# Last unit's single-quadrant products in two banks of their own, both last additions ahead of all copies, other units' sums folded in ahead of time

## Chip, cores, metric

One core of one Trainium2 chip. The metric is the device time of one execution in microseconds. Every run and every trace here is one execution of the whole program.

## The reference, cut to what matters

A gated recurrence over 4 sequences of 6,080 positions and 256 channels, then a two-layer block with `h - tanh(h)` between.

```python
def _attn_ref(x, f_logit, lower_bound):
    f = lower_bound + (1.0 - lower_bound) * sigmoid(f_logit)
    for t in range(S):
        h = f[:, t] * h + (1.0 - f[:, t]) * x[:, t]
        y[:, t] = h
    return y

def _moe_ref(x, w_in, w_out):          # x: (24320, 256), w_in: (256, 2048)
    h = x @ w_in
    g = h - np.tanh(h)
    return (g @ w_out).astype(np.float32)
```

## The kernel before

The program runs over 48 blocks of tokens (one of 256, then 512 each) and, in each, four units of 512 hidden channels. From the third block on, both layers use a fast matrix scheme with seven products in place of eight. The second layer's seven products are collected in four PSUM banks, `Qa` to `Qd`, over the four units; at the end of a block their sums are combined into the four quadrants `C[0]` to `C[3]` of the output, turned, and written. What the change touches is the end of the last block:

```python
PARTS = (
    (("Qa", 0, A11, "h", 0), ("Qa", 1, S1, "T", 0)),
    (("Qb", 0, A12, "h", 3), ("Qb", 1, S2, "h", 1)),
    (("Qc", 0, S3, "T", 1),),
    (("Qd", 0, S4, "h", 2), ("Qd", 1, A22, "T", 2)),
)

def finish(j, step):                       # p15, o1, o2, o3 (o4 only in other blocks)
    ...
    o, a, b = (
        None,
        (C[:, 0:2], acc[j, 1][:, :, 0:hb], twice(0)),
        (C[:, 2], acc[j, 2][:, 0, 0:hb], C[:, 1]),
        (C[:, 1:4:2], C[:, 1:3], twice(1)),
        (C[:, 1:3], acc[j, 3][:, :, 0:hb], C[:, 1:3]),
    )[step]
    nc.vector.tensor_tensor(out=o, in0=a, in1=b, op=ALU.add)

def end(j):                                # the last block's o4 and output
    ...
    for half in range(2):
        slot, r = ((2, 1), (1, 0))[half]
        nc.vector.tensor_tensor(
            out=C[:, slot], in0=acc[j, 3][:, r, 0:hb], in1=C[:, slot], op=ALU.add
        )
        name = ("Qa", "Qb")[half]
        bank = ps_b.tile([P, 2, KC, P], FP32, name=name, tag=name)
        for i in range(2):
            for k in range(KC):
                nc.tensor.transpose(
                    bank[:, i, k], C[:, 2 * k + half, i * P : (i + 1) * P], ident[:]
                )
        rows = osb[:, 2 * half : 2 * half + 2]
        (nc.scalar.copy, nc.vector.tensor_copy)[half](
            out=rows.rearrange("p i (m k) -> p i k m", k=KC), in_=bank[:]
        )
        t0 = starts[j] + half * hb
        nc.sync.dma_start(out=out[t0 : t0 + hb, :].rearrange(...), in_=rows)
```

The polynomial in place of `tanh` holds only for small arguments. The program therefore collects a flag, and after the fast path every engine reads the flag and jumps over a second, general path, which is unrolled over all 48 blocks. With these inputs the flag is zero and the path is never taken:

```python
fast()
seen = nc.values_load(flag[:].bitcast(INT32), ...)
with tc.If(seen != 0):
    general()
```

## Time and profile before

| | kernel before |
|---|---|
| median of the first 3 runs | 2330.94 us (2330.39 to 2331.64) |
| span of the profiled execution | 2330.1 us |
| TensorE busy | 2318.8 us, at full clock |
| last product of TensorE ends | 2322.83 us |
| from there to the end of the span ("tail") | 7.28 us |

The lines of the profile are in the prediction. In this trace TensorE has no gap between the opening (the first 12 us) and its last product, so only the 7.28 us behind that product can be won.

### The profile page before, as it was taken

What the parts mean: (1) busy time and instruction counts of PE and PEld (TensorE: products, weight loads), DVE (VectorE), ACT (ScalarE), POOL (GpSimd) and SP (SyncE); (2) the same over time, 40 slices, a digit from 0 to 9 for tenths busy, and PEclk for the clock granted to TensorE, in tenths of its full rate; (3) what the DMA queues carried; (4) which work ended last, traced back from release to release, by engine and by line L of the source; (5) the groups of instructions that cost most, each with busy time, mean ns of one, the idle gap of its engine ahead of it and who ended that gap; (6) DMA issues with size and microseconds to landing.
All of it is one profiled execution on the core that took longest, in us unless ns stands there. A gap on an engine that the chain in (4) does not pass through costs nothing.

```text
span 2330.1 us, 28649 instructions
## 1 busy us (share of the span) xinstructions
PE 2318.8 (100%) x10676; PEld 2025.3 (87%) x10676; DVE 2121.3 (91%) x2447; ACT 1800.6 (77%) x2686; POOL 0.7 (0%) x6
## 2 busy tenths in 40 slices
PE   9999999999999999999999999999999999999998
PEld 5888888888888888888888888888888888888887
DVE  8999899998999989999899999999899998999987
ACT  7777777777777777787777777777777777777775
POOL 0000000000000000000000000000000000000000
PEclk9999999999999999999999999999999999999999
DMA  6311211112111111111111121111211112111101
GB/s 172 64 23 29 45 37 28 28 33 41 37 28 28 37 37 37 28 28 40 33 37 28 28 44 30 37 28 28 46 28 37 28 28 46 31 33 28 28 10 29
DMA packets 296948, 85.05 MB, mean 36 GB/s; under 512 B 289888, under 2 KB 292704, under 8 KB 296800
## 3 DMA queue, kind: packets, MB, share of 16 engines
q1 hardware_dynamic: 296512, 82.87, 16.9%
q8 instruction: 85, 1.39, 0.3%
q14 instruction: 63, 0.52, 0.1%
q10 hardware_dynamic: 288, 0.26, 0.0%
HBM read 58.20 MB, written 24.90 MB: 36 GB/s over the span
## 4 chain that ended last, share of the span: by engine, by line
PE 99%; DMA 0%; DVE 0%; issue 0%; ACT 0%; SPq 0%
PE A L388 27%; PE Qd L471 14%; PE Qa L471 14%; PE D L388 14%; PE Qb L471 14%; PE B L388 7%; PE Qc L471 7%; PE A L687 1%; PE Qc L754 1%; PE Qa L754 1%; PE Qb L754 1%; PE D L687 0%; PE Qd L687 0%; PE B L687 0%; DMA fn<-in_f_logit_dram 0%; PE Qa L687 0%
## 5 line engine op out<-in xcount | busy, mean ns | idle before, releaser
L388 PE MATMUL A<-T,w_in 128*128 128x256 f32 x2208 | 558.8, 379 | 0.0
L388 PEld LDWEIGHTS A<-T,w_in 128*128 128x128 f32 x2208 | 419.5, 190 | 57.0
L432 DVE TENSOR_TENSOR h<-h,q 128x1024 f32<-128x1024 f32 x368 | 437.6, 1220 | 3.1
L426 DVE SCALAR_TENSOR_TENSOR q<-q,t 128x1024 f32<-128x1024 f32 x368 | 440.0, 1216 | 0.0
L419 ACT ACTIVATE q<-t 128x1024 f32<-128x1024 f32 x368 | 382.8, 1053 | 46.7 <-DVE h L432 43.8
L416 ACT ACTIVATE t<-h 128x1024 f32<-128x1024 f32 x368 | 388.6, 1056 | 3.1 <-DVE h L403 0.3
L437 ACT ACTIVATE junk<-t 128x1024 bf16<-128x1024 f32 x368 | 388.1, 1055 | 1.5
L451 DVE TENSOR_TENSOR Tg<-h 128x1024 f32<-128x1024 f32 x368 | 348.0, 946 | 6.4
L471 PE MATMUL Qb<-h,w_out 128*128 128x256 f32 x1472 | 347.7, 379 | 0.0
L471 PEld LDWEIGHTS Qb<-h,w_out 128*128 128x128 f32 x1472 | 279.7, 190 | 38.0
L471 PE MATMUL Qd<-h,w_out 128*128 128x256 f32 x736 | 219.0, 379 | 0.0
L471 PE MATMUL Qa<-Tg,w_out 128*128 128x256 f32 x736 | 219.0, 379 | 0.0
L471 PE MATMUL Qa<-h,w_out 128*128 128x256 f32 x736 | 218.9, 379 | 0.0
L471 PE MATMUL Qd<-Tg,w_out 128*128 128x256 f32 x736 | 218.9, 379 | 0.0
L400 ACT COPY h<-B 128x512 f32<-128x512 f32 x184 | 106.9, 581 | 143.0 <-PE B L388 94.2
L400 ACT COPY h<-A 128x512 f32<-128x512 f32 x184 | 107.2, 583 | 136.7 <-PE A L388 125.3
L403 DVE TENSOR_TENSOR h<-D,r 128x512 f32<-128x512 f32 x184 | 126.9, 689 | 92.7 <-PE D L388 89.1
L403 DVE TENSOR_TENSOR h<-A,r 128x512 f32<-128x512 f32 x184 | 126.3, 687 | 73.8 <-PE A L388 42.1
L400 ACT COPY r<-A 128x512 f32<-128x512 f32 x184 | 107.2, 583 | 105.9 <-PE A L388 105.9
L388 PE MATMUL D<-T,w_in 128*128 128x256 f32 x736 | 188.9, 379 | 0.0
L388 PE MATMUL A<-y,w_in 128*128 128x256 f32 x736 | 188.9, 379 | 0.0
L388 PE MATMUL B<-y,w_in 128*128 128x256 f32 x736 | 188.9, 379 | 0.0
(120 smaller groups left out, 3069.2 us busy)
## 6 DMA issues: line engine op xcount, KB each, us to landing
xn<-in_x_dram SPq DMA_DIRECT2D x184, 128.0 KB, 3.3
fn<-in_f_logit_dram SPq DMA_DIRECT2D x184, 128.0 KB, 3.1
out_dram<-osb SPq DMA_DIRECT2D x180, 128.0 KB, 2.8
raw<-in_moe_w_out_dram SPq DMA_DIRECT2D x8, 512.0 KB, 4.9
raw<-in_moe_w_in_dram SPq DMA_DIRECT2D x7, 512.0 KB, 4.7
out_dram<-osb SPq DMA_DIRECT2D x3, 256.0 KB, 3.9
fn<-in_f_logit_dram SPq DMA_DIRECT2D x1, 512.0 KB, 7.3
xn<-in_x_dram SPq DMA_DIRECT2D x1, 512.0 KB, 8.2
```

The source lines that it names most:

```text
L388: nc.tensor.matmul(ps[:, c], lhsT=w_in[u][:, slot, c * P : (c + 1) * P], rhs=mixes[j][right], start=start and c == 0, stop=True, skip_grou ...
L400: nc.scalar.copy(out=dst, in_=piece(n, bank))
L403: nc.vector.tensor_tensor(out=piece(n, "h")[:, q], in0=piece(n, bank), in1=piece(n, r), op=ALU.add)
L416: nc.scalar.activation(out=half(n, i, "t"), in_=half(n, i), func=AF.Square)
L419: nc.scalar.activation(out=half(n, i, "q"), in_=half(n, i, "t"), func=AF.Square, scale=RA, bias=RB,)
L426: nc.vector.scalar_tensor_tensor(out=q, in0=q, scalar=RC, in1=t, op0=ALU.add, op1=ALU.mult)
L432: nc.vector.tensor_tensor(out=h, in0=h, in1=q, op=ALU.mult)
L437: nc.scalar.activation(out=junk[:, :, :, 0 : st[n]["hb"]], in_=t, func=AF.Relu, bias=-TINY, accum_out=flags[:, 2 * n + i : 2 * n + i + 1],)
L451: nc.vector.tensor_tensor(out=o, in0=a, in1=b, op=ALU.subtract)
L471: nc.tensor.matmul(acc[j, part][:, r, 0 : st[n]["hb"]], lhsT=w_out[u][:, slot, c * P : (c + 1) * P], rhs=piece(n, right)[:, q, c], start=( ...
L687: nc.tensor.matmul(h[c], lhsT=w_in[u][:, 2 * k + s, c * P : (c + 1) * P], rhs=ys[j][:, k, 0:nb], start=k == 0 and (c == 0 or len(banks) == 2),
L754: nc.tensor.matmul(acc[j][i // 2][:, i % 2].rearrange("p (k m) -> p k m", k=2), lhsT=plain[j, u][:, s, c, i * P : (i + 1) * P], rhs=w_out[ ...
```

## The change

The intent: make the last two additions start as early as possible. The last unit's two products that go into only one quadrant each (`A22`, `S4`) get a PSUM bank each, so that the addition of the first can start while TensorE is still on the second. The other units' sums in `Qd` are copied out before and folded in before the end. Both last additions stand ahead of all copies, and the copies out are halved and spread over four banks and two engines. The diff, cut to its core:

```diff
+        def part_end(j, step):
+            p, kept = acc[j, "p"][:, :, 0:hb], acc[j, "kept"]
+            if step == "o1":
+                finish(j, 1)
+            if step == "p15":
+                nc.vector.tensor_tensor(
+                    out=kept[:, 2], in0=p[:, 1], in1=kept[:, 0], op=ALU.add
+                )
+                return
+            for o, a, b in {
+                "o1": (),
+                "o2": ((kept[:, 3], acc[j, 2][:, 0, 0:hb], C[:, 1]),),
+                "o3": (
+                    (C[:, 2], kept[:, 3], kept[:, 1]),
+                    (C[:, 1], C[:, 1], kept[:, 2]),
+                    (C[:, 3], kept[:, 3], p[:, 1]),
+                ),
+            }[step]:
+                nc.vector.tensor_tensor(out=o, in0=a, in1=b, op=ALU.add)
 ...
         def end(j):
+            alone = [ps_a.tile([P, TB], FP32, name="A", tag="A")[:, 0:hb] for _ in range(2)]
+            for half, (slot, right, q) in enumerate(((A22, "T", 2), (S4, "h", 2))):
+                for c in range(2):
+                    nc.tensor.matmul(
+                        alone[half],
+                        lhsT=w_out[NU - 1][:, slot, c * P : (c + 1) * P],
+                        rhs=piece(n, right)[:, q, c],
+                        start=c == 0,
+                        stop=c == 1,
+                    )
             for half in range(2):
-                slot, r = ((2, 1), (1, 0))[half]
+                slot = 2 - half
                 nc.vector.tensor_tensor(
-                    out=C[:, slot], in0=acc[j, 3][:, r, 0:hb], in1=C[:, slot], op=ALU.add
-                )
-                name = ("Qa", "Qb")[half]
-                bank = ps_b.tile([P, 2, KC, P], FP32, name=name, tag=name)
+                    out=C[:, slot], in0=alone[half], in1=C[:, slot], op=ALU.add
+                )
+            for half in range(2):
                 for i in range(2):
-                    for k in range(KC):
+                    name = ("Qa", "Qb", "Qc", "D")[2 * half + i]
+                    bank = ps_b.tile([P, KC, P], FP32, name=name, tag=name)
+                    for k in (0, 1) if half == 0 else (1, 0):
                         nc.tensor.transpose(
-                            bank[:, i, k], C[:, 2 * k + half, i * P : (i + 1) * P], ident[:]
+                            bank[:, k], C[:, 2 * k + half, i * P : (i + 1) * P], ident[:]
                         )
-                (nc.scalar.copy, nc.vector.tensor_copy)[half](
-                    out=rows.rearrange("p i (m k) -> p i k m", k=KC), in_=bank[:]
-                )
+                    (nc.scalar.copy, nc.vector.tensor_copy)[i](
+                        out=osb[:, 2 * half + i].rearrange("p (m k) -> p k m", k=KC),
+                        in_=bank[:],
+                    )
 ...
+                    if final and (name, u) == ("Qd", NU - 2):
+                        kept = mixpool.tile([P, 4, HB], FP32, name="T")
+                        acc[j, "kept"] = kept
+                        nc.scalar.copy(
+                            out=kept[:, 0:2], in_=acc[j, 3][:, :, 0 : sizes[j] // 2]
+                        )
```

More of the change, by code (lines that the diff above doesn't have):

```diff
@@ L521, in give @@
                 )
+        def part_end(j, step):
+            hb = sizes[j] // 2
+            p, kept = acc[j, "p"][:, :, 0:hb], acc[j, "kept"]
[6 more added lines that the diff above has]
+                return
+            C = acc[j, "C"][:, 0 : 4 * hb].rearrange("p (n t) -> p n t", n=4)
+            for o, a, b in {
[8 more added lines that the diff above has]
+                nc.vector.tensor_tensor(out=o, in0=a, in1=b, op=ALU.add)
@@ L523, in end @@
         def end(j):
-            hb = sizes[j] // 2
+            hb, n = sizes[j] // 2, j * NU + NU - 1
             C = acc[j, "C"][:, 0 : 4 * hb].rearrange("p (n t) -> p n t", n=4)
             osb = opool.tile([P, NQ, D], FP32, name="osb", tag="osb")
+            alone = [ps_a.tile([P, TB], FP32, name="A", tag="A")[:, 0:hb] for _ in range(2)]
[8 more added lines that the diff above has]
+                    )
@@ L540, in end @@
                         )
-                rows = osb[:, 2 * half : 2 * half + 2]
-                (nc.scalar.copy, nc.vector.tensor_copy)[half](
-                    out=rows.rearrange("p i (m k) -> p i k m", k=KC), in_=bank[:]
-                )
+                    (nc.scalar.copy, nc.vector.tensor_copy)[i](
+                        out=osb[:, 2 * half + i].rearrange("p (m k) -> p k m", k=KC),
+                        in_=bank[:],
+                    )
                 t0 = starts[j] + half * hb
@@ L546, in end @@
                 nc.sync.dma_start(
-                    out=out[t0 : t0 + hb, :].rearrange("(i p) d -> p i d", p=P), in_=rows
+                    out=out[t0 : t0 + hb, :].rearrange("(i p) d -> p i d", p=P),
+                    in_=osb[:, 2 * half : 2 * half + 2],
                 )
@@ L903, in fast @@
                         continue
+                    final = j == NBLK - 1
+                    if final and (name, u) == ("Qd", NU - 1):
+                        continue
                     if u is None:
-                        if (name, j) == ("o1", NBLK - 1):
+                        if final and name == "o1":
                             nc.vector.reduce_max(
@@ L908, in fast @@
                             )
-                        if j == NBLK - 1 and name in ("o4", "otr"):
-                            if name == "o4":
-                                end(j)
+                        if final and name == "o3":
+                            sum_up()
+                        if final and name == "o4":
+                            end(j)
+                        if final and name[0] == "o":
+                            if name in ("o1", "o2", "o3"):
+                                part_end(j, name)
                             continue
-                        if (name, j) == ("o3", NBLK - 1):
-                            sum_up()
                         steps[name](j)
@@ L917, in fast @@
                             fetch(j + 1)
+                        if final and name == "p15":
+                            part_end(j, name)
                         continue
                     steps[name](j * NU + u)
+                    if final and (name, u) == ("Qd", NU - 2):
[4 more added lines that the diff above has]
+                        )
     @with_exitstack
```

## The prediction

> **What bounds the kernel now.** I read the page first: the busy time of each engine, then the granted clock in 40 slices.
>
> ```profile
> span 2330.1 us, 28649 instructions
> PE 2318.8 (100%) x10676; PEld 2025.3 (87%) x10676; DVE 2121.3 (91%) x2447; ACT 1800.6 (77%) x2686; POOL 0.7 (0%) x6
> PEclk9999999999999999999999999999999999999999
> ```
>
> TensorE is busy for all but 11 us at full clock, so only fewer matmuls, or less time in which nothing is left to multiply, can help. The change takes no matmul away before the last unit. It can only touch the tail, so I read the table of windows next, with a cut at 2322.85 us, where the last product ends (columns: stretch, its length, busy us of PE, PEld, DVE, ACT, POOL with counts, clock, DMA share, GB/s).
>
> ```profile
> 2315.00:2322.85 7.85, 7.85 (x38) 6.41 (x36) 5.97 (x9) 0.73 (x2) 0.00 (x0) 1.00 0.31 68
> 2322.85:2330.10 7.25, 1.14 (x8) 0.73 (x7) 1.45 (x3) 0.62 (x1) 0.00 (x0) 0.91 0.26 84
> ```
>
> Up to 2322.85 TensorE has no gap; 7.25 us follow. That is everything the change can win from, 0.3% of the time. The chain that ended last says what lies in it (start, length, what):
>
> ```profile
> 2320.91 1.94 PE Qd L471 x8
> 2322.85 0.02 issue
> 2322.87 0.44 DVE C L531
> 2323.31 0.04 issue
> 2323.35 0.55 PE Qa L538 x3
> 2323.90 0.51 PE Qb L538 x4
> 2324.41 0.02 issue
> 2324.44 0.69 DVE osb L542
> ```
>
> The products into bank Qd end; both last additions, each 256 columns, read that bank; transposes into Qa, then into Qb; the second copy out. From there the transfer view and the view of the DMA queue's waits take over:
>
> ```profile
> out_dram<-osb SPq DMA_DIRECT2D x2, 256.0 KB, 3.9
> SPq L1046 <- DMA out_dram<-osb: 2.0, 2, 1.4
> ```
>
> The records give the two issues at 2324.58 and 2325.16, just behind the copies that end at 2324.56 (ACT) and 2325.13 (DVE). The second transfer lands at 2329.04, and 1.07 us of closing waits and barriers make 2330.11. So the end is: second copy done, then 3.9 us, then 1.07 us.
>
> Last, the timeline of VectorE and ScalarE just ahead of the end:
>
> ```profile
> 2320.02 0.69 DVE L503 TENSOR_TENSOR C<-Qb,p 128x512 f32<-128x512 f32 x1 [0.72 <-issue]
> 2320.83 0.42 DVE L503 TENSOR_TENSOR C<-Qc,C 128x256 f32<-128x256 f32 x1
> 2321.29 0.69 DVE L503 TENSOR_TENSOR C<-C,p 128x512 f32<-128x512 f32 x1
> 2322.87 0.76 DVE L531 TENSOR_TENSOR C<-Qd,C 128x256 f32<-128x256 f32 x2 [0.89 <-PE Qd L471]
> 2318.24 0.59 ACT L487 COPY p<-Qa 128x512 f32<-128x512 f32 x1 [5.20 <-PE Qa L471]
> ```
>
> VectorE idles 0.89 us before the last additions, ScalarE 5.2 us before its copy. There is room for added work in both.
>
> **What the Trainium skill says.** "PSUM — Partial Sum Buffer", section "PSUM bank collisions raise a hardware error", says that two engines must not touch one bank (same partitions) at once, even in disjoint columns, and wants waits guarded by bank. The trace agrees in effect: both sums of Qd are read only after its last matmul (2322.83), though the first matmuls for either half were done well before; the additions start at 2322.87 and 2323.21. "VectorE: DVE Perf Modes", section "The TRN2 errata", gives (N+151)/0.96 ns for an fp32 tensor_tensor add: 424 ns for 256 columns, 691 for 512. The trace has 425 and 415, 692 and 693: it agrees, and I use it for the added additions. [...] "Runtime: NRT & Kernel Launch", section "Instruction fetch mechanics", says that a taken branch outside the fetched pages has to fetch instructions by DMA. At the end each engine branches over the second code path; the trace has a 16,384-byte instruction packet from 2325.44 for 1.36 us amid the output transfers. That matters for a rival below.
>
> **The change part by part.** The order of the built program differs only in the last few dozen instructions; TensorE has the same count of products and transposes.
>
> (a) ScalarE copies Qd's sums of the first three units to SBUF. They are complete at about 2314.96 (last start 2314.58 plus 0.379); the copy is 0.59 us as L487's, done by 2315.7, in the idle 5.2 us. Cost on the path: 0.
>
> (b) VectorE adds p's second half to the kept sum (0.425 us) behind p's copy (2318.24+0.59 = 2318.83): 2318.87 to 2319.30. The reduction (0.54 us) moves to about 2319.24 to 2319.78. Its reader on TensorE comes only after Qc's products, at 2320.72: 0.9 us of slack. The addition of Qb waits for Qb's products anyway (2320.02). Cost 0.
>
> (c) After Qb (unchanged, ends 2320.71) and Qc (starts 2320.83, ends 2321.25), the 512-column addition becomes three of 256. The first starts as before at 2321.29; independent ones follow at 0.341 us, as the two of L531 do (2322.872 to 2323.213): 2321.29, 2321.63, 2321.97.
>
> (d) TensorE makes the same eight matmul passes, but the four of A22 first, into their own bank, then the four of S4. The first bank is done at the fourth start 2321.591 plus 0.379 = 2321.97, 0.86 us before the second (2322.83). The first last addition starts when VectorE is free: 2321.97+0.34 = 2322.31, ends 2322.74. In the kernel before it ended at 2323.30: 0.56 us won. The second runs 2322.87 to 2323.30; before, 2323.21 to 2323.63: 0.33 won.
>
> (e) Transposes now come in four groups of two. C[0] is ready early (2322.67 as before). C[2] follows the first addition by 0.053 us: 2322.79, ending 2323.12 (the 0.331 us of the first one after a wait). Qb's two end at 2323.34 (steps of 0.17 and 0.11 us, then 0.273). Qc's C[3] needs nothing; its C[1] waits for the second addition: 2323.35, ending 2323.68. D's end at 2323.90. Before, the last transpose ended at 2324.40: 0.50 won.
>
> (f) Copies are halved and paired across engines. ScalarE needs about 0.38 us for 256 columns (0.617 less 256 at 0.92 ns, the slope between 583 ns for 512 and 1055 for 1024), VectorE about 0.425. ScalarE: 2323.16 to 2323.54, 2323.72 to 2324.10. VectorE: 2323.38 to 2323.80, 2323.94 to 2324.36. So the first issue falls at 2323.83 instead of 2324.58, the second at 2324.39 instead of 2325.16: 0.75 and 0.77 us won. Of the 0.77, 0.50 are from additions and transposes, 0.27 from the shorter last copy.
>
> If transfer and closing keep their 3.9 and 1.07 us, the span falls by 0.77 us.
>
> **The rivals.** First, *the exit holds part of it back*. In the records, most of the output's packets are through by 2327.3, but a thin stream goes on until 2328.6, and a lone DMA engine's 32 packets of 46 ns make 1.5 us; it looks as if one engine began only after the instruction packet ended at 2326.79. TensorE's branch follows its last transposes' dispatch, which moves by only some 0.4 us (2323.74 to 2323.35). If that fetch sets the straggler, 0.4 us is won, not 0.77. Against it: transfers that start 0.75 us earlier have more packets through before the fetch. It makes 2330.5.
>
> Second, *VectorE's chain becomes the bound*. If the three additions do not overlap, each takes 0.46 us with its wait; the first last addition starts at 2322.69, the second at 2323.15 and ends 2323.57, close to before (2323.63). Then the split copies alone win, some 0.3 us: 2330.6. Against it: the built program has no wait between the three.
>
> Third, *noise or a new stall*. A new wait of TensorE on its own counter stands before the S4 products, but for a value reached dozens of matmuls earlier; four banks instead of two mean more semaphore hops (some 0.04 us each). If these eat everything: 2330.9, no change.
>
> **Range and chances.** I weigh the full 0.77 and the exit's 0.4 about equally: 0.6 us off the median of 2330.94, 2330.3 us. The three runs before spread over 1.25 us, twice the gain; with that and 0.3 us for the mechanism the range is 2329.4 to 2331.2. A gain of 2% would be 47 us, and the whole tail is 7.25: faster by over 2% is out of reach at 0.003. For slower there is no mechanism of that size: 0.007. Within 2%: 0.99.
>
> **What would show it.** In the profile after, the first last addition should start near 2322.31 and the second near 2322.87; the last copy should end near 2324.36; the issues should stand near 2323.83 and 2324.39; the stretch from the last product's end to the end of the span should be about 6.5 us instead of 7.25 (6.9 if the exit holds it). I am wrong if the additions of L546 stand 0.46 us apart, if TensorE shows a gap before 2322.8, if either copy takes as long as the 512-column one, or if the second transfer takes clearly longer than 3.9 us from issue to landing. A time below 2329.4 would mean that the exit shrank with it, which I have no reason to expect.

## The result, and the profile after

| | before | after |
|---|---|---|
| median of 6 runs | 2331.81 us (2330.39 to 2332.45) | 2331.66 us (2329.70 to 2332.48) |
| ratio | | 0.9999, 95% interval 0.9987 to 1.0012 |
| tail of the profiled execution | 7.28 us | 7.44 us |

Ratios are the mean time of one kernel's fast runs over that of the other's of the same rounds, so they are not quite the ratio of the medians. The prediction of 2330.3 us, with a range to 2331.2, missed: the time lies 0.5 us above the range.

The page after, its span and its busy times:

```profile
span 2330.3 us, 28654 instructions
PE 2319.1 (100%) x10674; PEld 2025.5 (87%) x10676; DVE 2121.6 (91%) x2451; ACT 1801.5 (77%) x2688; POOL 0.7 (0%) x6
```

VectorE's timeline after (start, length, engine, line, operation, idle time before it and its releaser):

```profile
2321.27 0.43 DVE L546 TENSOR_TENSOR C<-T 128x256 f32<-128x256 f32 x1
2321.61 0.42 DVE L546 TENSOR_TENSOR C<-C,T 128x256 f32<-128x256 f32 x1
2321.95 0.42 DVE L546 TENSOR_TENSOR C<-T,p 128x256 f32<-128x256 f32 x1
2322.28 0.41 DVE L566 TENSOR_TENSOR C<-A,C 128x256 f32<-128x256 f32 x1
2322.85 0.42 DVE L566 TENSOR_TENSOR C<-A,C 128x256 f32<-128x256 f32 x1 [0.16 <-PE A L557]
2323.33 0.42 DVE L577 COPY osb<-Qb 128x256 f32<-128x256 f32 x1
2323.92 0.42 DVE L577 COPY osb<-D 128x256 f32<-128x256 f32 x1 [0.16 <-PE D L574]
```

The engines did what the change wants. The first last addition starts at 2322.28, while TensorE is still on its last products (before: 2322.87). The chain that ended last, after:

```profile
2320.89 1.92 PE A L557 x8
2322.82 0.26 PE Qa L574 x2
2323.08 0.22 PE Qb L574 x2
2323.30 0.37 PE Qc L574 x2
2323.66 0.23 PE D L574 x2
2323.90 0.02 issue
2323.92 0.42 DVE osb L577
```

No addition stands on the chain any more, and the last copy ends at 2324.35, 0.78 us before the 2325.13 of the kernel before. But the windows table, cut at the last product's end, and the transfers of the kernel after say that nothing of it arrives:

```profile
2322.82:2330.26 7.44, 1.06 (x8) 0.66 (x7) 1.27 (x3) 0.77 (x2) 0.00 (x0) 0.72 0.26 83
```

```profile
out_dram<-osb SPq DMA_DIRECT2D x2, 256.0 KB, 4.5
```

```profile
SPq L1096 <- DMA out_dram<-osb: 2.6, 2, 2.0
```

The tail is 7.44 us in place of 7.28. The transfers take 4.5 us from issue to landing in place of 3.9, and the closing wait for them is 2.6 us in place of 2.0. What was won ahead of the transfers was given back in them.

**Where.** The DMA view can draw a window of 4 us in 40 slices of 0.1 us (GB/s in each). Both windows start 2.0 us after the last product's end. Before:

```profile
GB/s 0 0 0 82 0 82 215 236 317 297 225 287 369 328 307 338 440 307 287 297 338 277 92 61 51 61 41 51 51 31 21 113 20 20 31 20 31 10 0 0
```

After:

```profile
GB/s 0 0 133 338 266 256 236 307 379 451 359 328 348 307 297 317 277 133 62 82 61 51 72 82 41 72 61 123 51 31 31 20 21 31 20 20 31 20 102 0
```

Nearly all the output is through some 0.4 us earlier after the change: the high plateau starts and ends four slices sooner. Behind it comes a thin stream, mostly of 20 to 80 GB/s, and that ends at nearly the same time in both kernels: the last output packet at 5.78 us after the last product before, at 5.91 after. A packet of 1,024 bytes takes 46 ns in the records, that is 22 GB/s for one DMA engine: the last 0.9 us runs at the rate of a single engine. The landings say the same. (A transfer signals 16 times here, once for each DMA engine's share of it; each signal is called a landing.) In the first transfer after the change, 15 of 16 have come by 4.8 us after the last product, the last one comes at 5.70; in the second, the last comes at 6.37.

What else happened there: amid the output the records hold one packet of 16,384 bytes of queue 8, kind "instruction", from 2.92 to 4.28 us after the last product (before: 2.60 to 3.96). The DMA view after has its row:

```profile
q8 instruction: 1, 0.02, 2.1%
```

Queue 8 is TensorE's instruction stream: 85 packets of 256 instructions make 21,760, TensorE has 21,420 records, and a median of 256 of them lie between one packet and the next. This one is taken to belong to TensorE's jump over the general path. The jump is in the view of its source line (duration in ns) with 3.85 us before:

```profile
L1016 PEldq COMPARE_BRANCH  x1: 3847/3847/3847, 2324.4 to 2324.4; - x1
```

and 4.63 us after:

```profile
L1066 PEldq COMPARE_BRANCH  x1: 4627/4627/4627, 2323.9 to 2323.9; - x1
```

"Runtime: NRT & Kernel Launch", section "Instruction fetch mechanics", says that a taken branch beyond the fetched pages forces such a fetch; the trace agrees. The same 4 us also hold four (before) and five (after) packets of 8,192 bytes of queue 14, also "instruction", and a few other landings are late too (4.80, 5.25 and 5.44 us in the second transfer after). Which of these packets delays which landing was not tested by itself; e12 below adds a queue 8 packet alone.

So the theory: one DMA engine has to bring TensorE's instructions; its share of the output waits until that packet is through, and its last landing sets the end. The rivals: the two transfers are slower by themselves when they are issued closer together (0.51 us apart, 0.58 before), or the first trace is an unlucky draw and the gain is usually there.

In the tables below, times are counted from the end of the last product, as read in the records of each trace.

### The profile page after: what moved, and what is told of

It is laid out like the page before. It is cut to its first block, busy times and chain, and to the rows that moved or that the text cites. A ratio compares the mean times of both kernels' runs of the same rounds, so it can differ in the third digit from the quotient of the medians.

```text
span 2330.3 us, 28654 instructions
## 1 busy us (share of the span) xinstructions
PE 2319.1 (100%) x10674; PEld 2025.5 (87%) x10676; DVE 2121.6 (91%) x2451; ACT 1801.5 (77%) x2688; POOL 0.7 (0%) x6
## 4 chain that ended last, share of the span: by engine, by line
PE 99%; DMA 0%; SPq 0%; issue 0%; DVE 0%
PE A L388 27%; PE Qa L471 14%; PE Qb L471 14%; PE D L388 14%; PE Qd L471 14%; PE Qc L471 7%; PE B L388 7%; PE A L724 1%; PE Qa L791 1%; PE Qc L791 1%; PE Qb L791 1%; PE D L724 0%; PE Qd L724 0%; DMA xn<-in_x_dram 0%; PE B L724 0%; PE A L557 0%
## 5 line engine op out<-in xcount | busy, mean ns | idle before, releaser
L388 PE MATMUL D<-y,w_in 128*128 128x256 f32 x736 | 188.9, 379 | 0.0
```

The costliest lines, as they stand in the source:

```text
L388: nc.tensor.matmul(ps[:, c], lhsT=w_in[u][:, slot, c * P : (c + 1) * P], rhs=mixes[j][right], start=start and c == 0, stop=True, skip_grou ...
```

## The experiments

The readings below come from one trace each.

### e1 and e2: both kernels without the test and the general path

```diff
     fast()
-    seen = nc.values_load(flag[:].bitcast(INT32), ...)
-    with tc.If(seen != 0):
-        general()
```

> The kernel before without the test of the flag and the second code path, so no engine has to jump and no engine fetches a far page at the end. Theory (the exit's instruction fetches hold back one DMA engine's share of the output): issue to last landing of the second transfer falls from 3.9 us to 3.0 us or less, the thin stream of 1,024-byte packets at the end (2327.3 to 2328.6 in the kernel before) is gone, and the span falls by 1 us or more against the kernel before. Rival (the transit is a property of the two overlapping transfers alone): issue to landing stays at 3.9 us, within 0.2.

> The changed kernel without the test of the flag and the second code path. Theory: with the fetches gone the transit is the same as in the kernel before without them (within 0.2 us), so the 0.5 us by which the changed kernel issues earlier reaches the end: from the last product's end to the last landing 0.5 us less than in the kernel before without exit, and its time 0.4 to 0.6 us lower. Rival (closer or smaller transfers are slower by themselves): the transit is again about 0.6 us longer than in its partner, and the two end at the same distance from the last product.

| | last copy ends | second issue | last landing | issue to landing | tail |
|---|---|---|---|---|---|
| before | 2.30 | 2.33 | 6.21 | 3.88 | 7.28 |
| after | 1.53 | 1.82 | 6.37 | 4.55 | 7.44 |
| e1, before without exit | 2.30 | 2.33 | 4.67 | 2.34 | 5.62 |
| e2, after without exit | 1.53 | 1.82 | 4.24 | 2.43 | 5.20 |

The same 4 us of the DMA view, from 2.0 us after the last product, for e1:

```profile
GB/s 0 0 0 0 0 0 102 348 338 348 297 307 389 348 359 328 348 358 348 328 358 256 82 0 0 0 0 0 0 0 0 0 0 0 0 0 0 0 0 0
```

and for e2:

```profile
GB/s 0 0 174 348 348 276 338 399 358 348 328 348 348 348 379 348 338 195 21 0 0 0 0 0 0 0 0 0 0 0 0 0 0 0 0 0 0 0 0 0
```

The thin stream is gone in both, no packet of queue 8 is left in this stretch, and the plateau of the changed kernel ends four slices earlier. All 16 landings of a transfer come within 0.23 us of each other. The transits differ by 0.09 us, not by 0.67, so the rival that the transfers themselves are slower falls. The tails, in the windows table, e1 first:

```profile
2321.03:2326.65 5.62, 1.16 (x8) 0.73 (x7) 1.45 (x3) 0.61 (x1) 0.00 (x0) 0.86 0.27 93
```

```profile
2321.32:2326.52 5.20, 1.06 (x8) 0.66 (x7) 1.28 (x3) 0.77 (x2) 0.00 (x0) 1.00 0.30 102
```

Without the exit the change is worth 0.42 us, nearly the 0.51 by which it issues earlier. Times, 5 runs each: medians 2330.19 and 2330.03 us, against 2331.73 for the kernel before; the intervals of the ratios (0.9981 to 1.0009 and 0.9981 to 1.0008) include 1, so the times alone show none of this. The expected difference of 0.4 to 0.6 us between the two times was not seen (0.16).

### e5 and e6: both kernels with a short second path

```diff
-            for j, nb in enumerate(sizes):
+            for j, nb in enumerate(sizes[:1]):
```

The second path is wrong here if it were ever taken; the outputs are right with these inputs.

> The kernel before, with the second path cut to its first block of 48 (so it would be wrong if it were ever taken; it is not with these inputs), so that the test and the jump stay but the jump is short. Theory (the far jump's fetch holds one DMA engine): fewer or no 16,384-byte packet amid the output, issue to landing of the second transfer 2.3 to 2.8 us instead of 3.9, and from the last product's end to the end of the span about 5.7 us instead of 7.28. If a short jump fetches as a far one does, nothing changes: 7.1 to 7.4 us.

> The changed kernel with the second path cut to its first block. Theory: issue to landing 2.3 to 2.8 us instead of 4.55, and from the last product's end to the end of the span 0.4 to 0.5 us less than in its partner before with the short path: about 5.3 us instead of 7.44. If the jump, whatever its length, costs the same, 7.3 to 7.5 us.

| | TensorE's jump | its 16,384-byte packet | last landing | tail |
|---|---|---|---|---|
| e5, before, short | 1.55 to 1.92 | 2.65 to 4.03 | 6.17 | 7.60 |
| e6, after, short | 1.12 to 1.48 | 2.24 to 3.58 | 5.72 | 7.15 |

The jump itself shrinks to 0.37 us, as the theory says, but the absolute numbers missed: one 16,384-byte packet still comes, issue to landing stays at 3.85 and 3.90 us (expected: 2.3 to 2.8), and the closing after the landing takes 1.43 us in place of 1.07, so the tails are 7.60 and 7.15 us where 5.7 and 5.3 were expected. This miss is worth more than a hit. TensorE no longer waits for the packet, yet the landing does: it comes 2.14 us behind the packet's end in both. In e5, 15 of the first transfer's 16 landings come by 3.93 us and one at 5.54. So it is not TensorE's late arrival at the end that holds the output, it is the packet. The difference of the two tails, 0.45 us, is as expected.

### e12: a fetch without a jump

The changed kernel without test and general path, with filler on TensorE behind the last copy so that an ordinary fetch falls amid the output:

```diff
-            K1.7 df.0 ce.0 ... sg0.0 cb.0 K1.4
+            df.0 ce.0 ... sg0.0 cb.0
 ...
+            nc.tensor.matmul(late[:, 0:1], lhsT=ident[:], rhs=osb[:, 3, 255:256], ...)
+            for _ in range(150):
+                nc.tensor.matmul(late[:, 0:2], lhsT=zeros.bitcast(BF16)[:, 0:P],
+                                 rhs=zeros.bitcast(BF16)[:, 0:2], ...)
```

> The changed kernel without test, jump and second path, but with 150 tiny filler products on TensorE behind the last copy (and 11 fewer warming products in the opening, so that a boundary of 256 instructions falls into the filler). It puts an ordinary instruction fetch of TensorE amid the output, without any jump. Theory (it is the fetch, not the jump or the flag, that holds one DMA engine): a 16,384-byte packet within 1 to 3 us after the last product, and the last landing 2.1 to 2.25 us behind its end, if that end is later than about 2.2 us after the last product, with one landing of 16 over 1 us behind the rest; without the fetch (its partner) it was 4.24. The span gets longer by the filler, some 5 to 10 us, on purpose. Rival (jump or flag reads slow the transfers): landing stays at 4.2 to 4.3.

The DMA view of the same 4 us, with the row of the instruction queue:

```profile
GB/s 0 0 174 358 328 297 307 389 348 359 328 359 328 533 307 317 317 164 31 0 0 0 10 10 10 10 0 10 10 31 20 31 20 0 0 0 0 0 0 0
...
q8 instruction: 1, 0.02, 1.5%
```

The packet came, from 3.33 to 4.28 us. The last landing is at 5.78 in place of 4.24, and again it is one landing: the other 15 of the second transfer come by 4.45. No jump, no reading of the flag and no second path is in this program, so the rival that blames them falls. The filler as such does not slow the transfers either: the other landings of the second transfer come as in e2 (4.02 to 4.21 and 4.45 us, there 4.06 to 4.24). Two numbers of the expectation missed. The landing follows the packet's end by 1.50 us, not 2.1, and the filler made the tail 6.7 us, (5.20 without it), not longer by 5 to 10. The first has a reason that fits: this packet started 1.1 us after the output's first packets, so the first transfer's 16 packets of that engine were through (all its landings by 3.72) and only the second's remained: 15 output packets start behind the packet's end. 32 packets at 46 ns are 1.47 us, 16 are 0.74; 0.6 to 0.9 us remain in either case.

### e9, e10, e13, e14: the two kernels again

No edit.

> The changed kernel unaltered, for a second trace. Theory: in the tail the last landing follows the end of TensorE's 16,384-byte instruction packet by 2.1 to 2.25 us, as in the four traces with one such packet amid the output (2.25, 2.09, 2.14, 2.14), not the second issue by a fixed time; of 16 landings of the first transfer one or a few come over 1 us behind the rest. From the last product's end to the end of the span 7.1 to 7.6 us; the last copy ends 1.53 us after the last product, within 0.03. Rival (the first trace was an unlucky draw and the gain is usually there): 6.8 us or less.

> The kernel before unaltered, for a second trace. Theory: the same rule, landing 2.1 to 2.25 us behind the end of the packet; from the last product's end to the end of the span 7.1 to 7.6 us, so no more than 0.3 us from the changed kernel. The last product's own end may differ by up to 1.8 us between executions, from the opening alone.

> Third trace of the kernel before. Theory (the end is set by the end of TensorE's 16,384-byte packet, which starts 1.0 to 1.15 us behind TensorE's jump at 1.55 us after the last product and takes 1.2 to 1.4 us when it is not held up): landing about 6.2 us and end of the span about 7.25 us after the last product; held up, more. Rival (the two kernels' tails are the same on average): 7.1.

> Third trace of the changed kernel. Theory: TensorE's jump at 1.12 us after the last product, so the packet ends at about 3.45, landing at about 5.7 and the end of the span at about 6.8 us after the last product, 0.45 us less than the kernel before, unless the packet is held up as in the first trace (7.44). Rival (same on average): 7.1 or more.

Their rows of the windows table: e10, then e13 (before), then e9, then e14 (after):

```profile
2322.82:2330.63 7.81, 1.16 (x8) 0.73 (x7) 1.45 (x3) 0.61 (x1) 0.00 (x0) 0.88 0.25 78
```

```profile
2323.18:2330.14 6.96, 1.16 (x8) 0.73 (x7) 1.45 (x3) 0.62 (x1) 0.00 (x0) 0.71 0.27 87
```

```profile
2321.89:2328.67 6.78, 1.06 (x8) 0.66 (x7) 1.27 (x3) 0.77 (x2) 0.00 (x0) 0.87 0.29 91
```

```profile
2321.58:2328.79 7.21, 1.07 (x9) 0.67 (x7) 1.28 (x3) 0.77 (x2) 0.00 (x0) 0.91 0.28 85
```

| | jump starts | packet | last landing | landing behind packet's end | tail |
|---|---|---|---|---|---|
| before | 1.55 | 2.60 to 3.96 | 6.21 | 2.25 | 7.28 |
| e10 before | 1.55 | 2.66 to 4.62 | 6.73 | 2.12 | 7.81 |
| e13 before | 1.55 | 2.57 to 3.81 | 5.89 | 2.08 | 6.97 |
| after | 1.11 | 2.92 to 4.28 | 6.37 | 2.09 | 7.44 |
| e9 after | 1.14 | 2.16 to 3.37 | 5.72 | 2.35 | 6.79 |
| e14 after | 1.11 | 2.45 to 3.88 | 6.14 | 2.26 | 7.21 |

The issue stands at the same distance from the last product in all traces of one kernel (2.32 to 2.33, and 1.82). The tail does not: it spreads over 0.84 us in one kernel and 0.65 in the other. The landing follows the packet's end by 2.08 to 2.35 us in all six, and the end of the span follows the landing by 1.07 us in all six. That is the rule that holds; the distance from the second issue, 3.57 to 4.55 us, is not.

The packet's own end varies with when it starts (1.02 to 1.81 us behind the jump) and how long it takes (1.21 to 1.96 us). The means of the tails are 7.35 us before and 7.15 after; with three traces each and spreads of that size, 0.2 us apart is no finding. The tails set down beforehand were missed more often than met: e9's 6.79 us is the number of its rival, the unlucky draw (6.8 or less; theory 7.1 to 7.6); e10's 7.81 lies above its theory's 7.1 to 7.6; e13's 6.97 is neither 7.25 nor 7.1; e14's 7.21 is its rival's (7.1 or more; theory 6.8 unless held up). So the average stays undecided, and that the first trace was just an unlucky draw is not ruled out; that the gain is there in full (6.5 us) is seen in none of the three.

### e3, e4, e8: three attempts to move one side alone

e3 adds 16 filler products behind the last transposes, to push TensorE's jump past the output.

```diff
                             end(j)
+                            for _ in range(16):
+                                nc.tensor.matmul(late[:], lhsT=zeros..., rhs=zeros..., ...)
```

> The changed kernel with 16 filler products on TensorE after its last transposes (about 3.4 us at 0.216 us), so that TensorE jumps at about 2327.4 instead of 2323.9 and its 16,384-byte instruction packet comes after the output. Theory: the second transfer lands about 3.0 us after its issue (about 2327.6) instead of 4.55 (2329.18); the span still ends later, at about 2332, because TensorE's own jump then ends last. Rival (the transit is the transfers' own): landing stays 4.5 us behind the issue, at about 2329.2.

The design failed. The jump started at 1.46 us, not at 4.6: TensorE's sequencer reached it while the products were still queued. The filler brought a second 16,384-byte packet (2.19 to 4.85 and 2.51 to 3.81), and the last landing came at 7.15 us, 2.30 behind the later end; 11 of the second transfer's 16 landings had come by 4.34, the other five between 6.30 and 7.15. Median of 4 runs 2332.69 us. It speaks for the packet, but not in the way planned.

e4 puts two idle additions on VectorE ahead of its copies, so that both transfers are issued later.

```diff
+            for i in range(2):
+                nc.vector.tensor_tensor(out=idle[:, i], in0=zeros[:], in1=zeros[:], op=ALU.add)
             for half in range(2):
                 for i in range(2):
```

> The changed kernel with two idle additions of 512 columns (about 1.3 us) on VectorE ahead of its two copies, so that both output transfers are issued 0.7 to 1.0 us later (second at about 2325.4 instead of 2324.63). Theory (the issue is off the path; the DMA engine that serves the fetch ends last): the last landing and the span move by less than 0.3 us. Rival (issue to landing is fixed at 4.55 us): landing and span move by the full 0.7 to 1.0 us.

The second issue came 1.05 us later (2.87), and the last landing did not move (6.23 against 6.37), nor did the tail grow (7.30 against 7.44). That meets the theory's number. It is weaker evidence than it looks: the packet ended at 3.43, so the landing is 2.80 us behind it, and the second issue took 1.26 us in place of 0.40. Here the late issue itself had come close to setting the end.

e8 splits each transfer by partitions into 0 to 103 and 104 to 127, to leave some DMA engines without output.

```diff
-                nc.sync.dma_start(out=..., in_=osb[:, 2 * half : 2 * half + 2])
+                for q, (a, e) in ((nc.sync, (0, 104)), (nc.scalar, (104, P))):
+                    q.dma_start(out=...[a:e], in_=osb[a:e, 2 * half : 2 * half + 2])
```

> The changed kernel, complete, with each output transfer split into partitions 0 to 103 from SP and 104 to 127 from ScalarE's queue, sizes that 16 engines cannot share evenly, so that some DMA engines should get no output at all. Theory, if the engine that serves TensorE's fetch is one of those left out: the last landing comes at about 4.5 us after the last product instead of 6.37, and the end is then set by TensorE's jump (5.8 us), so the span ends about 0.5 us earlier. If it is among those that still serve output, landing stays near 6.3 us. Rival (no engine is special): landing moves by less than 0.3 us too.

Inconclusive. The last landing came at 5.86, which lies among the 5.72 to 6.37 us of the unaltered kernel, 2.41 us behind a packet that ended at 3.46, with late landings in both kinds of transfer, so the engine of the fetch was not among those left out, or there is more than one. ScalarE, now an issuer, made its first step behind its jump only at 6.28 us and set the end: tail 7.24 us.

### e7, e11: why the first issue came 0.3 us late

The prediction had the first issue at 2323.83; it stood at 2324.12, though both copies had ended by 2323.76. In e7 the engines of the copies are swapped, in e11 each half's copies are on one engine; both are without the second path.

```diff
-                    (nc.scalar.copy, nc.vector.tensor_copy)[i](
+                    (nc.vector.tensor_copy, nc.scalar.copy)[i](       # e7
+                    (nc.scalar.copy, nc.vector.tensor_copy)[half](    # e11
```

> The changed kernel without the second path, and with the two engines of the copies out swapped, so that ScalarE makes the later copy of each pair. It tests why the first transfer is issued 0.33 us behind its last copy (1.31 us after the last product, where the copy ends at 0.94). Theory: the issue itself carries only the wait for ScalarE, and the wait for VectorE stands in an instruction of its own ahead of it; when that one ends last, the issue starts 0.33 us later. With ScalarE last, the first issue stands within 0.05 us of the copy's end (about 0.95 us after the last product) and the last landing comes at about 3.95 us instead of 4.24. Rival (a fixed cost of the first issue after a long pause): the issue again starts 0.33 us behind the last copy.

> The changed kernel without the second path, with both copies of the first half on ScalarE and both of the second on VectorE, so that each output transfer waits for one engine and carries that wait itself. Theory (the 0.33 us before the first issue is the start of a transfer instruction behind a wait instruction that ended only then; three runs showed 0.333 behind that wait's end): the first issue stands within 0.05 us of its last copy's end, about 1.07 us after the last product instead of 1.31. Rival (any first issue after a pause starts late): 0.33 us behind the copy, about 1.37.

In the built program each transfer carries one wait itself; the second stands in a wait instruction ahead of it. In the changed kernel that one is the wait for VectorE. The records show the transfer's start 0.333 us behind that instruction's end in the kernel after. In e7 the issue came at 1.16 us: the expected 0.95 missed, and so did the rival's 0.33 behind the last copy (1.25). But VectorE's copy ended at 0.794, and 0.033 us of signal plus 0.333 make 1.16: it is again 0.333 behind the end of the wait instruction, whichever copy is last. In e11, where the transfer waits for one engine, the first issue stands at 1.00 us, 0.025 behind the copy's end at 0.973. Its last landing is at 3.92 us and its tail the shortest of all (one trace):

```profile
2321.53:2326.41 4.88, 1.07 (x9) 0.67 (x7) 1.18 (x3) 0.67 (x2) 0.00 (x0) 1.00 0.31 107
```

The second issue, whose landing was to end the span, was late because the first was: its wait instruction could only start at 1.76 us, behind the first issue, and the transfer followed that instruction by 0.029 us, as it no longer had to wait (the copy had ended at 1.53).

In e7 the landing was expected at 3.95 us and came at 4.32, one landing 0.25 us behind the others, with an 8,192-byte instruction packet from 2.11 to 2.42 beside the transfers' start.

### e15, e16: the version that e11 points to, complete

The edit of e11 in the complete kernel, with test and general path.

> The changed kernel, complete, with both copies of the first half on ScalarE and both of the second on VectorE, which without the second path brought the issues 0.31 and 0.15 us forward and the landing to 3.92. Theory (the issue is off the path, the packet sets the end): tail as the changed kernel's, 6.8 us, within 0.2 unless held up. Rival (the issue sets the end): 0.2 to 0.3 us shorter than the changed kernel's. The time against the kernel before cannot tell them apart: the opening alone moves it by up to 1.8 us.

> The same kernel as the run ahead of it, for a second trace; the same expectations: theory 6.8 us from the last product to the end of the span, rival 0.2 to 0.3 us less than the changed kernel's.

The issues stood at 1.00 and 1.67 us, as in e11. The packet ran from 2.14 to 4.08 in one trace and from 3.06 to 4.35 in the other, the landings came at 6.30 and 6.51 us (2.22 and 2.17 behind), the tails were 7.37 and 7.59 us. Earlier issues brought nothing in these two traces: the rival that the issue sets the end falls. The theory's 6.8 us missed too; both packets ended late. Median of 5 runs 2331.20 us against 2330.72 before, ratio 1.0001 (0.9987 to 1.0015). It was not timed beside the changed kernel, and its tails (7.37 and 7.59) are no shorter than that one's (6.79 to 7.44).

## Why the prediction was wrong

**What it got right.** The way to the last copy, to within 0.03 us. From the last product's end, predicted and measured: first last addition -0.52 and -0.53, second 0.04 and 0.04; last transpose ends 1.07 and 1.07; last copy ends 1.53 and 1.53. ScalarE's 256-column copy was put at 0.38 and took 0.39; the three additions overlapped, so the second rival (VectorE's chain as the bound) did not happen. The cost of (a) and (b) on the path was 0.

**The issue, mis-sized.** "So the first issue falls at 2323.83 instead of 2324.58, the second at 2324.39 instead of 2325.16: 0.75 and 0.77 us won." The issues came 0.46 and 0.52 us earlier in their traces. The term left out is the 0.333 us between the end of a wait instruction that had to wait and the transfer behind it (e7, e11 and the trace after); the first issue paid it, and the second came late behind the first. The order of the built program showed both waits; they were not priced.

**The transit, the step that failed.** "If transfer and closing keep their 3.9 and 1.07 us, the span falls by 0.77 us." The closing kept its 1.07 us in all six traces. The transfer did not: 4.55, 3.90 and 4.32 us from the second issue to the landing in the three traces of the changed kernel. 3.9 us is not a property of the transfer, which takes 2.3 to 2.4 us without the fetch (e1, e2). It is the distance to another event, the end of TensorE's instruction packet plus about 2.2 us. In two of the three traces the second transfer took clearly longer than 3.9 us, which the prediction had named as a sign of being wrong. It saw the cause as its first rival, gave it half the weight in its number, and argued against it: "transfers that start 0.75 us earlier have more packets through before the fetch". They had not: the times fit one engine's share of both transfers (32 packets, 1.47 us) coming behind the packet as a whole; from the packet's end to the last output packet it is 1.82 us before and 1.64 after.

**How much of the rival's 0.4 us is there.** The jump moved by 0.44 us, as the rival had it, and between e5 and e6 the landing moved by 0.45. Between the two kernels themselves the mean of three landings moved by 0.20 us (6.28 to 6.08), and single pairs range from 1.02 us earlier to 0.47 later. In two of three traces of the changed kernel the packet ran late (it ended 2.77 and 3.17 us behind the jump's start, against 2.23 in the third and 2.26 to 3.07 before). A possible reason is that the earlier output is already in that engine's queues when the fetch arrives. The traces agree with it: where the packet started at least 0.06 us ahead of the first output packet (before, e13, e9, e4) it ended 2.23 to 2.41 us behind the jump's start, where it started at least 0.2 us behind that (after, e14, e15, e16) 2.77 to 3.24. But no run moved this alone, so it is argued, not shown.

**The base, mis-sized too.** The prediction took 0.6 us off a median of three runs. The 34 executions of the kernel before have a mean of 2331.38 us with a standard deviation of 0.97, and run from 2329.64 to 2333.35; the first three were low. In the six runs of the result its median was 2331.81, so a gain of 0.6 us would only just have reached the range. The 8 executions of the changed kernel have a mean of 2331.23. The scatter ahead of the tail comes from the opening: in the 18 traces the last product ends anywhere from 2321.0 to 2323.2 us, but from ScalarE's 101st instruction (at 79.2 to 81.4 us) to that end it is 2241.80 us in every one, within 0.01. A change of 0.4 us cannot be read from so few times that scatter like this; the tail in the traces can carry it, and there too it is half buried.

**What stays open.** Whether the complete changed kernel is shorter by a few tenths on average (0.2 us in the means of three traces each), why the packet sometimes starts 0.7 us late or takes 0.7 us longer, and what in the opening makes the 2 us.

## What to carry to other kernels

When the last transfer sets the end, find what its last landing follows before you shorten the way to its issue: draw the bandwidth in slices, and if a thin stream of one engine's rate trails the plateau, look for instruction packets beside it. A jump at the end of this program put such a packet amid the output, whether it was long or short; without test and jump the tail was 1.7 us shorter of 7.28 in one kernel and 2.2 of 7.44 in the other (one trace each). Price the waits of a transfer too: one that waited for a single engine started 0.025 us behind it, one behind a wait instruction that had to wait 0.333 us behind that one's end.

## What the Trainium skill lacked or had wrong

- "DMA: Bandwidth & Descriptors", section "Anatomy of one DMA — SWDGE (gpsimd) path", gives its fit of fixed and variable time for transfers issued through GpSimd; the output here is issued by SyncE, and no page has such a fit for that. The runs show 2.3 to 2.4 us from issue to landing for the second of two overlapping transfers of 256 KB when no instruction packet runs beside it (e1, e2), and 3.57 to 4.55 us when one of TensorE's does.
- No page says that an instruction fetch holds back one DMA engine's share of a data transfer. The runs show a last landing 2.08 to 2.35 us behind the packet's end in six traces, and 1.50 us when only the second transfer's share was still to come (e12).
- No page gives the time from the end of a wait to the start of a transfer on SyncE's queue. The runs show 0.025 us from the awaited copy's end where the transfer carries the wait, and 0.333 us from the end of a wait instruction ahead of it that had to wait.
- "Runtime: NRT & Kernel Launch", section "Instruction fetch mechanics", names the stall of a far branch but gives no size. The runs show 3.65 to 4.63 us for TensorE's jump over the general path in the six traces of the two kernels, and 0.37 us over a short one.
